# In the first batch the GpSimd queue loads the values ahead of the weights

## The chip, the cores and the metric

One core of one Trainium2 chip. The metric is the device time of one execution, in microseconds (us); lower is better. The traced execution of the kernel before took 487.22 us (span on the core 485.4). Times inside a trace count from the start of its span. The granted clock is the share of its full clock that TensorE was given.

## The reference

Cosine attention (8 batches, 12 heads, 448 positions, head size 64), then a feed-forward block with exact GELU on the 3584 x 768 result:

```python
q_n = q / (norm(q) + 1e-6);  k_n = k / (norm(k) + 1e-6)
attn = softmax(q_n @ k_n.T / tau)
x = (attn @ v)                        # to [3584, 768]
h = x @ w_in                          # 768 x 2048
out = (0.5 * h * (1 + erf(h / sqrt(2)))) @ w_out    # 2048 x 768
```

Inputs and output are float32. The kernel multiplies in bf16.

## The kernel before

The kernel handles two heads at a time (a "group"; six per batch, 48 in all). While TensorE works on attention of batch b, it fills its gaps with the second product of batch b - 1. In batch 0 there is no such work, so it runs dummy matmuls ("spin") to keep its clock up. Tile names in the profile: qk (q and k), sq (squares), rn (reciprocal norms), qkb (scaled q and k in bf16), tp and qkT (transposed), st (scores), pt (their exponentials), sm (sums), o (attention times v), hp (first product), op (second product), wi and wo (the two weights).

v, wi and wo are cast from float32 to bf16 as they are loaded; all of these loads go out on the GpSimd queue. q and k go out on the SyncE queue (one on ScalarE's).

```python
def load_v(g):                      # 112 KB
    nc.gpsimd.dma_start(out=t, in_=v[b, 2*p:2*p+2].rearrange(...))

def load_wi(i):                     # 768 KB each, four of them
    nc.gpsimd.dma_start(out=wi[:, r:r+n, c], in_=moe_w_in[...].rearrange(...))

def scale(g):                       # q half and k half
    for i, eng in enumerate((nc.vector if g == 0 else nc.gpsimd, nc.gpsimd)):
        eng.tensor_tensor(qkb[:, i]..., t[:, i], rn[:, i]..., ALU.mult)

def attention(b, fill):
    for i in range(HP):             # HP = 6 groups of this batch
        g = b * HP + i
        scores(g, 0)                # (if i == 0 and b > 0: done earlier)
        if b == 0:
            upto(scale, min(i + 2, HP)); roots(min(i + 3, HP + 1))
            upto(square, min(i + 4, HP + 1))
            spin(7 if i == 0 else 3)
        if i > 0:
            sums_one(g - 1)         # batch 0
            values(g - 1, ...)      # o: needs v of group g - 1
        scores(g, 2)
        if b == 0: spin(5 if i == 0 else 2)
        if i < HP - 1: transposes(g + 1)
        if b == 0:
            upto(reduce, min(i + 4, HP + 1))
            upto(load_wi, min(i + 2, 4))
        upto(load_v, g + (3 if b == 0 else 4))
        ...                         # cut

# start of the kernel (cut)
spin(24)
upto(square, 1); upto(reduce, 1); roots(1); upto(square, 2)
upto(scale, 1)
upto(load_v, 1)
upto(load_wi, 1)
upto(reduce, 2); roots(2); transposes(0); spin(5)
...
```

`upto(f, n)` calls f for every index below n that is not yet done.

## Time and profile before

| | before |
|---|---|
| device time, median of 3 runs | 486.55 us (486.14 to 487.27) |
| TensorE busy | 464.7 of 485.4 us (96%) |
| GpSimd busy | 256.7 us (53%) |
| ScalarE busy | 299.1 us (62%) |
| mean granted TensorE clock | 0.989 |

The averages hide where time can be won; the prediction below reads that from the waits and the timelines. In a line of waits stand the total us, how often, and the longest. A line of a timeline gives the start and the length in us, the engine (PE is TensorE, POOL GpSimd, ACT ScalarE, DVE VectorE), the line of the kernel, the operation, what it writes and reads, and how many; a bracket at its end gives the engine's idle time just before it and what ended that. One view is added here, the table of windows of 5 us of the kernel before. Its columns are the window, its length, busy us (and instructions) of PE, PEld, DVE, ACT and POOL, then the granted clock, the DMA share (the time that packets took, as a share of 16 engines' span; it can read above 1) and GB/s.

```profile
20.00:25.00 5.00, 2.73 (x23) 1.26 (x23) 2.63 (x4) 4.03 (x8) 4.83 (x6) 1.00 1.11 235
25.00:30.00 5.00, 0.57 (x4) 0.36 (x6) 0.25 (x1) 0.17 (x1) 4.82 (x6) 0.77 1.19 242
30.00:35.00 5.00, 4.28 (x26) 1.82 (x20) 1.24 (x3) 1.72 (x2) 1.64 (x2) 0.50 1.16 238
35.00:40.00 5.00, 5.00 (x32) 2.12 (x29) 1.30 (x2) 3.83 (x7) 2.50 (x3) 0.70 1.12 235
```

See three things. TensorE is all but idle from 25 to 30 us. The clock is low not in the idle window alone but for the two after it. And GpSimd (the last busy column) is full up to 30 us and has time afterwards.

### The profile page before, as it was taken

What the parts mean: (1) busy time and instruction counts of PE and PEld (TensorE: products, weight loads), DVE (VectorE), ACT (ScalarE), POOL (GpSimd) and SP (SyncE); (2) the same over time, 40 slices, a digit from 0 to 9 for tenths busy, and PEclk for the clock granted to TensorE, in tenths of its full rate; (3) what the DMA queues carried; (4) which work ended last, traced back from release to release, by engine and by line L of the source; (5) the groups of instructions that cost most, each with busy time, mean ns of one, the idle gap of its engine ahead of it and who ended that gap; (6) DMA issues with size and microseconds to landing.
All of it is one profiled execution on the core that took longest, in us unless ns stands there. A gap on an engine that the chain in (4) does not pass through costs nothing.

```text
span 485.4 us, 8032 instructions
## 1 busy us (share of the span) xinstructions
PE 464.7 (96%) x3266; PEld 236.3 (49%) x3266; DVE 156.2 (32%) x228; ACT 299.1 (62%) x447; POOL 256.7 (53%) x248
## 2 busy tenths in 40 slices
PE   8758999999999999999999999999999999999995
PEld 5324454445544555445544555444544555445563
DVE  5323513623153232523145231532144231331021
ACT  4838657774766557775676557875566656885400
POOL 4957908947382835668192744849094472411000
PEclk9969999999999999999999999999999999999999
DMA  9998964672056612664056520575046400331022
GB/s 207 237 238 148 204 94 95 138 187 90 7 110 170 172 37 44 137 144 138 0 101 167 142 85 11 122 183 147 0 90 170 101 20 2 65 106 34 1 65 65
DMA packets 48982, 51.87 MB, mean 107 GB/s; under 512 B 3833, under 2 KB 43825, under 8 KB 48945
## 3 DMA queue, kind: packets, MB, share of 16 engines
q1 hardware_dynamic: 31424, 39.34, 29.4%
q0 software_dynamic: 17280, 11.80, 17.2%
q8 instruction: 25, 0.41, 0.3%
q10 hardware_dynamic: 240, 0.23, 0.1%
q14 instruction: 13, 0.10, 0.1%
HBM read 52.04 MB, written 11.11 MB: 130 GB/s over the span
## 4 chain that ended last, share of the span: by engine, by line
PE 87%; ACT 4%; DMA 3%; POOL 2%; issue 2%; DVE 0%; POOLq 0%; ACTq 0%
PE op L244 30%; PE hp L365 29%; PE st L173 8%; PE o L183 8%; PE tp L162 5%; PE sm L204 3%; DMA v<-in_v_dram 3%; PE sm L216 3%; ACT ln L194 2%; POOL qkb L150 1%; ACT g L389 1%; PE spin L291 1%; DMA qk<-in_k_dram 1%; ACT pt L176 1%; POOL wi L266 0%
## 5 line engine op out<-in xcount | busy, mean ns | idle before, releaser
L176 ACT ACTIVATE pt<-st 112x896 bf16<-112x896 f32 x192 | 164.9, 911 | 42.2 <-PE st L173 41.8
L244 PE MATMUL op<-wo,g 128*128 128x384 bf16 x896 | 160.1, 326 | 0.0
L365 PE MATMUL hp<-x,wi 128*128 128x448 bf16 x768 | 149.1, 352 | 0.5
L389 ACT ACTIVATE g<-hp 128x448 bf16<-128x448 f32 x128 | 66.9, 545 | 74.5 <-PE hp L365 73.9
L244 PEld LDWEIGHTS <-g 128*128 128x128 bf16 x896 | 81.8, 98 | 62.0 <-issue 14.6
L365 PEld LDWEIGHTS <-wi 128*128 128x128 bf16 x768 | 74.1, 98 | 72.1 <-issue 5.4
L150 POOL TENSOR_TENSOR qkb<-qk,rn 112x512 bf16<-112x512 f32 x95 | 97.2, 1049 | 11.1 <-DVE rn L141 10.8
L117 POOL TENSOR_TENSOR sq<-qk 112x1024 f32<-112x1024 f32 x45 | 84.5, 1892 | 0.4
L129 DVE TENSOR_REDUCE nq<-sq 112x16 f32<-112x1024 f32 x47 | 57.1, 1216 | 45.9 <-POOL sq L117 45.7
L139 POOL TENSOR_SCALAR se<-sr 112x48 f32<-112x48 f32 (+2 forms) x18 | 5.5, 308 | 117.8 <-ACT sr L137 117.6
L173 PE MATMUL st<-qkT 64*112 64x448 bf16 x384 | 59.1, 377 | 4.2 <-DVE qkT L163 3.1
L230 POOL TENSOR_TENSOR x<-os,rb 128x448 bf16<-128x448 f32 x28 | 31.2, 1133 | 50.7 <-DMA rb<-rows 41.8
L248 DVE COPY ot<-op 128x384 f32<-128x384 f32 x56 | 30.8, 550 | 77.5 <-PE op L244 75.5
L183 PE MATMUL o<-pt,v 112*64 112x448 bf16 x384 | 45.8, 361 | 5.9 <-DMA v<-in_v_dram 5.9
L163 DVE COPY qkT<-tp 128x896 bf16<-128x896 bf16 x48 | 29.9, 623 | 65.3 <-PE tp L162 65.2
L194 ACT ACTIVATE ln<-sm 128x448 f32<-128x448 f32 x34 | 18.3, 538 | 35.3 <-PE sm L204 21.9
L173 PEld LDWEIGHTS <-qkT 64*112 64x112 bf16 x384 | 19.6, 126 | 39.0 <-issue 30.0
L141 DVE RECIPROCAL rn<-se 112x48 f32<-112x48 f32 (+2 forms) x20 | 7.9, 393 | 86.9 <-POOL se L139 86.8
L104 POOL DMA_DIRECT2D v<-in_v_dram x48 | 34.0, 708 | 2.4 <-DMA rb<-rows 1.3
L183 PEld LDWEIGHTS <-v 112*64 112x64 bf16 x384 | 19.6, 111 | 25.7 <-issue 9.5
L162 PE MATMUL tp<-ident,qkb 112*128 112x112 bf16 x384 | 27.4, 215 | 3.3 <-POOL qkb L150 1.3
L162 PEld LDWEIGHTS <-qkb 112*128 112x128 bf16 x384 | 22.0, 99 | 17.2 <-issue 10.6
(31 smaller groups left out, 168.7 us busy)
## 6 DMA issues: line engine op xcount, KB each, us to landing
qk<-in_q_dram SPq DMA_DIRECT2D x48, 224.0 KB
qk<-in_k_dram SPq DMA_DIRECT2D x47, 224.0 KB
rb<-rows SPq DMA_DIRECT2D x28, 224.0 KB
v<-in_v_dram POOLq DMA_DIRECT2D x48, 112.0 KB, 3.1
wi<-in_moe_w_in_dram POOLq DMA_DIRECT2D x4, 768.0 KB, 13.5
wo<-in_moe_w_out_dram POOLq DMA_DIRECT2D x4, 768.0 KB, 15.1
out_dram<-ot SPq DMA_DIRECT2D x8, 336.0 KB
out_dram<-ot SPq DMA_DIRECT2D x8, 288.0 KB
```

The source lines that it names most:

```text
L104: nc.gpsimd.dma_start(out=t, in_=v[b, 2 * p:2 * p + 2].rearrange("h (p c) d -> p h (c d)", c=NC))
L117: nc.gpsimd.tensor_tensor(sq, t, t, ALU.mult)
L129: nc.vector.tensor_reduce(nq, sq, mybir.AxisListType.X, ALU.add)
L150: eng.tensor_tensor(qkb[:, i].rearrange("p c h d -> p h c d"), t[:, i], rn[:, i].to_broadcast([CS, 2, NC, D]), ALU.mult)
L162: nc.tensor.transpose(tp[:, i, c, :], qkb[:, i, c].rearrange("p h d -> p (h d)"), ident)
L173: nc.tensor.matmul(st[:CS, h, :S], lhsT=qkT[rows, 1, c, :], rhs=qkT[rows, 0, :, :], start=True, stop=True)
L176: nc.scalar.activation(pt, st[:CS, :, :S], AF.Exp, scale=inv_tau)
L183: nc.tensor.matmul(o[h * D:(h + 1) * D, :S], lhsT=v_t[g][:, h, c, :], rhs=pt_t[g, c][:, h, :], start=(c == 0), stop=(c == NC - 1))
L230: eng.tensor_tensor(x_t[b][:, p, :], os_t.pop(g), rb_t.pop(g), ALU.mult)
L244: nc.tensor.matmul(ps[:, :NH], lhsT=g_t[sb][:, kf, t * 128:(t + 1) * 128], rhs=wo[:, kf, ni * NH:(ni + 1) * NH], start=(kf == 0), stop=(kf ...
L365: nc.tensor.matmul(hps[m], lhsT=wi[:, kd, m * 128:(m + 1) * 128], rhs=x_t[b][:, kd, :], start=(kd == 0), stop=(kd == KD - 1))
L389: nc.scalar.activation(g_t[sb][:, m, hf * S:(hf + 1) * S], hps.pop(m), AF.Gelu)
```

## The change

The intent: values are small and needed soon, weights are large and needed after 50 us, and both are on one queue. So v0, v1 and v2 go out first. A tiny copy that reads q of group 0 holds v0 and v1 back until that load is in. In the loop v is asked for one group earlier and stands ahead of wi, and wi starts one iteration later.

```diff
             if b == 0:
                 upto(reduce, min(i + 4, HP + 1))
-                upto(load_wi, min(i + 2, 4))
-            upto(load_v, g + (3 if b == 0 else 4))
+            upto(load_v, g + 4)
+            if b == 0:
+                upto(load_wi, min(i + 1, 4))
@@ start of the kernel
     spin(24)
+    late = nrm.tile([CS, 1], F32, tag="late", name="late", bufs=1)
+    nc.gpsimd.tensor_copy(late, qk_t[0][:, 0, 1, NC - 1, D - 1:D])
+    upto(load_v, 2)
     upto(square, 1)
     ...
     upto(scale, 1)
-    upto(load_v, 1)
-    upto(load_wi, 1)
+    upto(load_v, 3)
```

## The prediction

> **What bounds the kernel now.** I read the page first. TensorE (PE) is busy for 96% of the span, so time can only be won where PE stands idle or runs slowly. The slices show where that is: of 40 slices of 12.1 us, only the first four are below 9 tenths, and the third (24 to 36 us) has a granted clock of 6 tenths.
>
> ```profile
> PE   8758999999999999999999999999999999999995
> PEclk9969999999999999999999999999999999999999
> DMA  9998964672056612664056520575046400331022
> ```
>
> Next the waits of PE over the whole span. One stands out, and it occurs once:
>
> ```profile
> PE o L183 <- DMA v<-in_v_dram: 5.9, 1, 5.9
> PE st L173 <- DVE qkT L163: 3.1, 5, 0.7
> PE spin L291 <- POOL ident masks.py:199: 1.3, 1, 1.3
> PE tp L162 <- POOL qkb L150: 1.3, 2, 0.9
> ```
>
> The timeline of PE places it. The product of group 1 with its values (o) starts 5.93 us late, at 29.43, and that group of eight then takes 1.70 us where the same eight take 0.92 us for the next head pair:
>
> ```profile
> 22.55 0.95 PE L204 MATMUL sm<-pt,ones 112*64 112x448 bf16 x8
> 29.43 1.70 PE L183 MATMUL o<-pt,v 112*64 112x448 bf16 x8 [5.93 <-DMA v<-in_v_dram]
> ...
> 38.07 0.92 PE L183 MATMUL o<-pt,v 112*64 112x448 bf16 x8
> ```
>
> The timeline of GpSimd (POOL) says why the values are late. POOL issues both the weights wi and the values v. The values of groups 1 and 2 are issued at 16.58, behind two 768 KB pieces of wi (issued at 9.85 and 15.75), and the tile view of v gives 12.8 and 13.5 us from their issue to landing; where nothing lies ahead of them (issue at 39.59) it gives 3.2 us.
>
> ```profile
> 9.85 0.80 POOL L266 DMA_DIRECT2D wi<-in_moe_w_in_dram  x1
> 10.65 2.07 POOL L150 TENSOR_TENSOR qkb<-qk,rn 112x512 bf16<-112x512 f32 x2
> ...
> 15.75 0.83 POOL L266 DMA_DIRECT2D wi<-in_moe_w_in_dram  x1
> 16.58 1.33 POOL L104 DMA_DIRECT2D v<-in_v_dram  x2
> 17.93 2.05 POOL L150 TENSOR_TENSOR qkb<-qk,rn 112x512 bf16<-112x512 f32 x2
> 20.07 0.25 POOL L139 TENSOR_SCALAR se<-sr 112x16 f32<-112x16 f32 x1
> 20.40 1.89 POOL L117 TENSOR_TENSOR sq<-qk 112x1024 f32<-112x1024 f32 x1
> ```
>
> The chain that ended last agrees: it runs over a piece of 12.80 us "DMA v" from 16.58 to 29.39.
>
> **What the Trainium skill says.** "DMA: Bandwidth & Descriptors", section "Queues, rings and completion order": on each DMA engine a queue's descriptors are consumed in ring order, and the engine goes round between queues that have work. The trace agrees: v behind two wi pieces takes 12.8 us, v alone 3.2 us. So order of issue on the POOL queue is the lever. The same page, "SWDGE vs HWDGE vs iDMA": a transfer that changes its type can only be issued from GpSimd; v and wi both go from float32 to bf16, so they share that queue and can only be reordered. "TensorE: Matmul & The Clock Gate", section "What's actually happening": after an idle window of about 3.4 us the matmul clock drops to half and it needs sustained work to come back. The trace agrees: the windows of 5 us have a granted clock of 0.77, 0.50 and 0.70 at 25 to 30, 30 to 35 and 35 to 40 us, and 1.00 on both sides.
>
> **The change part by part.**
>
> Added: one tiny copy on POOL that reads the last element of q of group 0, so it waits until that load is in (VectorE starts on it at 4.33). Then v0 and v1 are issued, 0.7 to 0.9 us each: POOL has done that by about 6.5, and its first real work (qkb of group 0) starts at 7.51. This lies in idle time and costs nothing. Their landing is needed at 17.70 (o of group 0) and 23.5 (o of group 1). The first loads compete with the q and k loads, but even the 8.4 us that v0 took in this crowd before puts them at about 13 and 15. In time.
>
> Moved: v2 follows scale of group 0 and the first wi is no longer there (9.05 to 10.65 now holds v0 and wi0). It moves into the loop, one wi in each of iterations 0 to 3. So iteration 3 now carries a wi issue (0.83 us) which it did not before.
>
> Removed: the wait of 5.93 us. With it goes the slow clock. Between 29.43 and 37.5 the groups ran at 1.70 (o), 0.99 (st), 0.99 (spin), 0.95 (tp), 0.99 (st), 1.37 (spin), 1.57 (sm); at full clock the timeline gives 0.92, 0.59, 0.59, 0.57, 0.59, 0.78, 0.95. The difference is 0.78 + 0.40 + 0.40 + 0.38 + 0.40 + 0.59 + 0.62 = 3.6 us. So 9.5 us are on the path, plus up to 0.6 from POOL waits.
>
> **But it is not all given back, because POOL becomes the pace of the first batch.** An iteration (score to score of the next group) takes PE and ScalarE 5.07 us when nothing disturbs it (41.13 to 46.20). POOL takes, from qkb to qkb, 23.76 - 17.93 = 29.59 - 23.76 = 5.83 us: two qkb 2.05, se 0.25, sq 1.89, wi 0.83, v 0.68, gaps 0.13. Until now the wait for v hid that. After the change POOL does the same work in iterations 1 to 3. Let me lay it out. se of group 2 stays at 13.59 (it waits for ScalarE). sq to 15.75, v3 and wi0 (0.70 + 0.83) to 17.3, qkb of group 2 to 19.4. Then 5.83 each: qkb of group 3 to 25.2, of 4 to 31.0, of 5 to 36.9. PE transposes each as it comes (tp of group 2 came right behind qkb at 20.04 before). PE's own pace from 19.6 would have been 24.7, 29.8, 34.9, so POOL is what ends last, by 0.5, 1.2 and 2.0 us. The transposes of group 5 start at 44.93 before and at 36.9 after: 8.0 us earlier. After that nothing in batch 0 needs POOL for PE, and the 7.5 us from there to the first hp matmul (52.45) stay: hp starts at 44.4.
>
> **Are the weights still there in time?** Behind one another a wi piece moves at the 0.16 MB/us that the software queue got between 17 and 25 us beside the q and k loads, so 0.786 MB in 4.9 us, less than the 5.83 us between issues. wi0 to wi3 are issued at about 16.5, 22, 28 and 34 and land by about 23, 29, 35 and 42. The first half of the columns (wi0, wi1) is needed at 44.4, the second half 48 matmuls of 0.19 us later, 53.5. The wo pieces, issued from 45.74 before, go out from about 39 and need 4 times 4.9 us: to about 62. The first half is needed at 71.85 - 8 = 64. So it holds. The rest of the kernel is PE at full clock with waits under 1 us, and it moves as one piece.
>
> The sum: 486.55 - 8.0 = 478.5 us, 1.6% less.
>
> **The rivals.**
>
> First: POOL does not bind, and the whole 9.5 us (or 10.1 with the waits for qkb) come back: 476.5 to 477. For it: the iterations from 41 us on run at 5.07 without a wait for POOL. Against it: POOL has no idle time from 13.6 to 31.6 in the timeline, apart from gaps under 0.1 us; in that stretch it is at its own pace.
>
> Second: a new DMA wait. The trace shows that under load the software queue moved nothing until about 14.9 us, though v0 was issued at 9.0, while q and k had all of the 235 GB/s. If v0 and v1 are held back in the same way, they land at about 17 to 18 and o of group 0 waits up to 1 us; or if they do share early, 2 times 112 KB (0.9 us each) push q and k of groups 2 and 3 back from 8.6 and 10.5 to some 10.4 and 13.2, right at their squares (9.77 and 13.92). Either would cost 0.3 to 1.5 us: 479 to 480.
>
> Third: wi, now 6 us later, is late for hp, or wo for the second product. By the count above there are 10 and 2 us of slack; if the DMA engines were slower than I think, PE would wait a few us and the clock might fall again: 482 to 485. DMA is not saturated from 40 to 50 us before (132 and 100 GB/s), which speaks against it.
>
> Fourth: the first batch's idle gaps, now 1.5 of 5.83 us, let the clock fall. PE had gaps of 0.39 + 0.72 us per iteration at 20 us and stayed at 1.00; I give it little.
>
> **Range and chances.** 478.5 is the POOL-paced case (some seven in ten). The free case is 2 us below, the small DMA costs 0.5 to 1.5 us above, the noise of a run about 0.5 us. Range 476.9 to 480.6. Faster by over 2% means below 476.8, which is about all that the wait, the clock and the POOL waits hold together: 0.06. Slower needs the weights to be late by far more than the slack: 0.01.
>
> **What would show each step.** Right: no wait of o for v; clock 9 in every slice from the second on; POOL without idle time from 13.6 to about 37 and PE waiting for qkb some 0.5 to 0.8 us before each tp of groups 3, 4 and 5; tp of group 5 near 36.9, hp near 44.4, and after that the same timeline shifted by 8. Wrong: a wait of hp for wi or of op for wo; a wait of sq for q or k, or of o for v, early on; iterations of 5.1 us with idle POOL, which is the free case.

## The result and the profile after

| | before | after |
|---|---|---|
| device time, median | 486.91 us (486.14 to 487.48, 4 runs) | 479.28 us (478.96 to 479.29, 4 runs) |
| ratio | | 0.9843 (95%: 0.9826 to 0.9860) |
| mean granted clock, traced run | 0.989 | 0.999 |
| first hp matmul | 52.45 us | 44.13 us |
| TensorE wait of o for v | 5.93 us | none |
| TensorE wait of tp for qkb | 1.3 us, 2 times | 3.6 us, 5 times |

1.6% faster. Of the 8.2 us between the two spans, 8.3 had been gained by the first hp matmul; the rest of the kernel is the same work.

The waits of TensorE over the whole span of the changed kernel (total, times, longest):

```profile
PE st L173 <- DVE qkT L163: 3.9, 6, 0.7
PE tp L162 <- POOL qkb L150: 3.6, 5, 1.1
PE spin L291 <- POOL ident masks.py:199: 1.3, 1, 1.3
PE sm L204 <- ACT pt L176: 0.4, 1, 0.4
```

The wait for v is gone from the list, and the wait of the transposes for GpSimd's scaling has grown by 2.3 us. Three waits in the timeline of TensorE of the changed kernel are 1.6 us of that; another of 1.08 us, before the transposes of group 0, cost nothing (they began at 8.97 us, at 9.10 before).

```profile
22.68 0.92 PE L183 MATMUL o<-pt,v 112*64 112x448 bf16 x8
...
25.07 0.57 PE L162 MATMUL tp<-ident,qkb 112*128 112x112 bf16 x8 [0.43 <-POOL qkb L150]
...
30.88 0.57 PE L162 MATMUL tp<-ident,qkb 112*128 112x112 bf16 x8 [0.57 <-POOL qkb L150]
...
36.71 0.57 PE L162 MATMUL tp<-ident,qkb 112*128 112x112 bf16 x8 [0.58 <-POOL qkb L150]
```

o of group 1 takes 0.92 us at full clock, right behind its sums. The transposes of groups 3, 4 and 5 stand 5.81 and 5.83 us apart. The timeline of GpSimd of the changed kernel has the same spacing and no gap for anything but its own work:

```profile
16.34 0.78 POOL L266 DMA_DIRECT2D wi<-in_moe_w_in_dram  x1
17.12 2.07 POOL L150 TENSOR_TENSOR qkb<-qk,rn 112x512 bf16<-112x512 f32 x2
19.27 0.25 POOL L139 TENSOR_SCALAR se<-sr 112x16 f32<-112x16 f32 x1
19.60 1.89 POOL L117 TENSOR_TENSOR sq<-qk 112x1024 f32<-112x1024 f32 x1
21.44 0.73 POOL L104 DMA_DIRECT2D v<-in_v_dram  x1
22.16 0.78 POOL L266 DMA_DIRECT2D wi<-in_moe_w_in_dram  x1
22.93 2.08 POOL L150 TENSOR_TENSOR qkb<-qk,rn 112x512 bf16<-112x512 f32 x2
```

Note how small the waits are beside what they stand for: 0.4 to 0.6 us each in the list, while the iteration is 0.76 us longer than the 5.07 us it takes undisturbed. A wait is counted only from the end that is modelled for the matmul before; the spacing of one operation from iteration to iteration is the safer reading.

And the windows of 5 us of the changed kernel, to set against those of before: no low clock, and GpSimd full throughout.

```profile
25.00:30.00 5.00, 4.22 (x37) 2.07 (x37) 2.63 (x4) 3.98 (x8) 4.83 (x7) 1.00 1.12 241
30.00:35.00 5.00, 3.71 (x33) 1.72 (x31) 2.63 (x4) 4.08 (x8) 4.83 (x6) 1.00 1.12 220
```

### The profile page after: what moved, and what is told of

It is laid out like the page before. It is cut to its first block, busy times and chain, and to the rows that moved or that the text cites. A ratio compares the mean times of both kernels' runs of the same rounds, so it can differ in the third digit from the quotient of the medians. Undisturbed runs are those within 1.5% of the kernel's fastest.

```text
span 477.2 us, 8032 instructions
## 1 busy us (share of the span) xinstructions
PE 460.2 (96%) x3266; PEld 234.6 (49%) x3266; DVE 156.6 (33%) x228; ACT 299.1 (63%) x447; POOL 257.6 (54%) x249
## 4 chain that ended last, share of the span: by engine, by line
PE 87%; ACT 5%; POOL 3%; DMA 2%; DVE 1%; issue 1%; POOLq 0%; ACTq 0%
PE op L244 31%; PE hp L366 30%; PE st L173 8%; PE o L183 8%; PE tp L162 5%; PE sm L204 3%; PE sm L216 3%; ACT ln L194 2%; DMA qk<-in_q_dram 2%; POOL qkb L150 1%; ACT g L390 1%; POOL sq L117 1%; ACT pt L176 1%; PE spin L291 1%; DVE qkT L163 0%
## 5 line engine op out<-in xcount | busy, mean ns | idle before, releaser
L163 DVE COPY qkT<-tp 128x896 bf16<-128x896 bf16 x48 | 29.9, 623 | 54.7 <-PE tp L162 54.4
```

## The experiments

The theory: order in the GpSimd queue made v1 late (5.93 us), the idle time then cost a slow clock (3.6 us), and GpSimd's own pace takes part of that back. The rivals: v was late because the DMA engines were full; the clock costs nothing of its own; GpSimd's waits only stand in for others. Eleven runs, five rounds each. e1 to e4 ran on one chip beside 11 runs of the kernel before (487.06 us median, 483.95 to 489.23), e5 to e8 on another (487.97, 484.74 to 489.25), the last three again on the first chip, later (486.87, 483.25 to 487.71, 5 runs).

### e1: the wait kept, the clock kept up

The kernel before, with

```diff
+                if g == 2:
+                    spin(28)
                 values(g - 1, not one)
```

> The kernel before, with 28 extra spin matmuls ahead of the product of group 1 with its values (28 times 0.195 = 5.5 us of work in the wait). The wait for v stays, only the clock is kept up. Theory (the loss was a wait of 5.93 us plus 3.6 us of half clock after it): the slow groups between 29.4 and 37.5 us go back to full clock, 3.6 us gained, 483.2 us; granted clock 0.99 or more. Rival (the clock costs nothing of its own, as GpSimd would set the pace in that stretch anyway): less than 1 us gained, 486 us.

Measured: 483.26 us median (483.15 to 483.65), ratio 0.9927 (0.9897 to 0.9958), granted clock 1.000. From the timeline of TensorE of e1:

```profile
23.19 5.50 PE L291 MATMUL spin<-blank,ident 112*112 112x448 bf16 x28
28.62 0.95 PE L183 MATMUL o<-pt,v 112*64 112x448 bf16 x8
...
48.10 12.88 PE L367 MATMUL hp<-x,wi 128*128 128x448 bf16 x66
```

5.5 us of useless matmuls make the kernel 3.8 us faster than the kernel before beside it (medians). o still starts 5.4 us after the end of its sums (22.31 + 0.95), but takes 0.95 us instead of 1.70. Not all of the 3.8 us need be the clock: in this execution v of group 1 had landed at 27.6 us (29.4 in the trace of the kernel before), so o waited for the spins, not for v, and started 0.8 us earlier. From o of group 1 to the first hp matmul the kernel before takes 23.02 us (29.43 to 52.45) and e1 19.48 us. So the slow clock is a cost of its own: 3.5 us by this stretch, 3.6 us by the sum of the stretched groups.

The second thing to see is the spread: 0.5 us for e1, 5.3 us for the kernel before in the same rounds. Over all 27 runs of the kernel before beside the experiments, the time rises as the mean granted clock falls: four runs at 0.993 or 0.996 average 484.6 us, six at 0.983 or 0.984 average 488.4. But fourteen runs at 0.989 lie anywhere from 484.69 to 488.45, so the clock is not all of it. The landing of v varies too, and the spins of e1 hide that. How much each contributes is not shown; these runs were not traced.

### e2: half of the scaling moved off GpSimd

The changed kernel, with

```diff
-        for i, eng in enumerate((nc.vector if g == 0 else nc.gpsimd, nc.gpsimd)):
+        for i, eng in enumerate((nc.vector if g < HP else nc.gpsimd, nc.gpsimd)):
```

> The changed kernel, with the q half of the scaling of groups 1 to 5 on VectorE instead of GpSimd. Theory (GpSimd paces the first batch at 5.83 us an iteration, which takes back some 2 us of the gain): GpSimd is lighter by 0.5 to 1.05 us an iteration, the waits of tp for qkb of groups 3, 4 and 5 go, iterations become 5.1 us, 1.5 to 2.2 us gained on the changed kernel, 477.1 to 477.8 us. Rival (the 0.4 to 0.6 us waits for qkb only replace waits for ScalarE that come right after): no gain, 479 us.

Measured: 477.16 us median (477.07 to 477.44), ratio 0.9801 (0.9771 to 0.9831). From the timeline of TensorE of e2:

```profile
24.63 0.56 PE L162 MATMUL tp<-ident,qkb 112*128 112x112 bf16 x8
...
29.70 0.56 PE L162 MATMUL tp<-ident,qkb 112*128 112x112 bf16 x8
...
34.88 0.56 PE L162 MATMUL tp<-ident,qkb 112*128 112x112 bf16 x8
```

No bracket, so no wait, and 5.07 and 5.18 us between them; hp starts at 42.29 against 44.13. GpSimd's pace was worth 2.1 us: the changed kernel gave 479.25 on the same chip later (the control below). One thing cost part of what was moved: with VectorE on the q half at the same time, GpSimd's k half takes 1.31 to 1.54 us where it took 1.04. The Trainium skill, "SBUF — State Buffer", section "🔬 SBUF: two separate sides", says that VectorE with two SBUF inputs and GpSimd share a port pair that one of them locks for a whole instruction. The longer times agree with that: VectorE's half (0.68 us) started first each time, and overlaps of 0.40, 0.64, 0.47 and 0.41 us went with 0.27, 0.50, 0.33 and 0.27 us more for GpSimd. That is an agreement, not a test of the cause.

### e3: two wi issues moved into GpSimd's idle time

The changed kernel, with wi0 issued after v2 and wi1 after the scaling of group 1:

```diff
+                if i == 0:
+                    upto(load_wi, 2)         # right after scale of group 1
...
-                upto(load_wi, min(i + 1, 4))
+                upto(load_wi, min(i + 2, 4) if i else 2)
...
     upto(load_v, 3)
+    upto(load_wi, 1)
```

> The changed kernel, with the first two pieces of wi issued in GpSimd's idle time before and after the scaling of group 1 (9.6 and 12.4 us), so that the loop holds two issues of wi and not four, still behind v0 to v2. Theory (GpSimd time paces iterations 1 to 3): 2 times 0.78 us less up to the scaling of group 5, transposes of group 5 at 35.2 instead of 36.7, 1.5 us gained on the changed kernel, 477.8 us. Rival (the pieces of wi, 6 us earlier, take DMA time from q and k of groups 3 and 4, or from v3): a wait of sq for q or k, or of o for v, and no gain or a loss, 479 us or more.

Measured: 477.99 us median (477.80 to 478.30), ratio 0.9818 (0.9788 to 0.9848). From the timeline of TensorE of e3:

```profile
30.33 0.57 PE L162 MATMUL tp<-ident,qkb 112*128 112x112 bf16 x8 [0.41 <-POOL qkb L150]
...
35.40 0.56 PE L162 MATMUL tp<-ident,qkb 112*128 112x112 bf16 x8
```

The transposes of group 5 come at 35.40, where 35.2 was expected (36.71 in the changed kernel). Issuing a transfer is work for GpSimd: two issues of 0.78 us out of the loop are 1.3 us off the kernel (medians, control below). wi0 and wi1 going out 6.6 and 9.6 us earlier hurt nothing: v0 to v2 were ahead of them, and no wait for v, q or k came in the loop.

### e4: only v0, v1 and v2 ahead of the first wi

The kernel before, with `upto(load_v, 1)` at the start turned into `upto(load_v, 3)` and nothing else.

> The kernel before with one part of the change alone: v0, v1 and v2 are issued ahead of the first piece of wi; the loop (a piece of wi, then v of three groups ahead) and the start are as before. Same bytes, about the same times, other order. Theory (order in the GpSimd queue made v1 late): o of group 1 does not wait; v3 and v4 are now behind pieces of wi, land at about 35 and 41, against a need at 34 and 40, so waits of 0 to 3 us in all, 479.5 to 483 us. Rival (the DMA engines were full, so v is late in any order): o of group 1 still waits 3 us or more, 484 us or more.

Measured: 480.87 us median (480.15 to 481.87), ratio 0.9881 (0.9847 to 0.9916). From the timeline of TensorE of e4:

```profile
22.95 0.92 PE L183 MATMUL o<-pt,v 112*64 112x448 bf16 x8
...
34.85 0.95 PE L183 MATMUL o<-pt,v 112*64 112x448 bf16 x8 [0.36 <-DMA v<-in_v_dram]
...
41.18 0.95 PE L183 MATMUL o<-pt,v 112*64 112x448 bf16 x8 [1.07 <-DMA v<-in_v_dram]
```

The same bytes, with the DMA engines as full, and o of group 1 does not wait: it was the order, not the load. (v1 and v2 are also issued some 7 us earlier here, which e4 alone does not separate from the order; e8 does.) v3 and v4, still behind pieces of wi, took 12.4 and 12.9 us to land; they were in at 34.8 and 41.1, as expected, and cost 0.4 and 1.1 us. This one line brings most of the gain; the rest of the change brings 1.6 us more (480.87 against 479.25, the control).

### e5: without the copy that holds v0 and v1 back

The changed kernel without the two `late` lines, so that v0 and v1 go out at 1.5 us.

> The changed kernel without the small copy that holds v0 and v1 back until q of group 0 is in: they are issued at about 1.4 us. Theory A (the copy is needed: v competes with q and k of groups 0 and 1, 2 times 112 KB): VectorE's first square (4.2 us) or ScalarE's square of group 1 (6.7 us) starts 0.5 to 1 us later, and all of the rest with it: 479.8 to 480.3 us. Theory B (under load the GpSimd queue first moves data about 5 us after the issue, as in both kernels, so v comes after group 0 anyway): start unchanged, 479.2 to 479.4 us.

Measured: 479.52 us median (479.29 to 480.61). In its trace VectorE's first square began at 4.66 us, against 4.20 in the changed kernel, which looked like theory A. So it was run again beside the control.

### e6: e2 and e3 together

> The changed kernel with both earlier experiments at once: the q half of the scaling on VectorE, and two wi issues in GpSimd's idle time. Theory (with the first of these GpSimd is no longer the bound, TensorE and ScalarE are, at 5.07 to 5.17 us an iteration): the two gains of 1.8 and 1.0 us do not add; 0.0 to 0.3 us better than the first alone, 476.9 to 477.2 us. Rival (GpSimd is still the bound): the second gain adds, 476.1 us or less.

Measured: 477.24 us median (477.16 to 477.54), against 477.16 for e2 on the other chip. The gains of 2.1 and 1.3 us do not add: both relax the same bound, and once it no longer binds the second is worth nothing. GpSimd now waits for ScalarE in every iteration (0.33 to 1.04 us). GpSimd's busy time from 15.7 to 36 us fell from 19.64 us in e2 to 17.18 us in e6, and hp started at 42.27 against 42.29.

### e7: e6 with fewer spins

```diff
-                spin(7 if i == 0 else 3)
+                spin(4 if i == 0 else 1)
...
-                spin(5 if i == 0 else 2)
+                spin(1)
```

> The same with both, and most of the idle spin matmuls of the first batch taken out (7, 5, 3 and 2 become 4, 1, 1 and 1). Theory (what paces the first batch now is ScalarE, busy 4.8 us of 5.07, with TensorE's spins filling its waits[...]): 0.7 to 1.7 us gained on the kernel with both, 475.4 to 476.4 us, clock 0.99 or more. Rival (the spins keep the clock up): the granted clock falls in the first batch and the time rises to 478 us or more.

Measured: 475.39 us median (475.21 to 475.61, 5 runs), ratio 0.9748 (0.9722 to 0.9775), granted clock 1.000: 1.85 us better than e6, a little more than the range expected. This is the fastest version, and the only one clearly more than 2% faster than the kernel before. From the table of windows of e7, its four iterations from the scores of group 1 to those of group 5 (columns as above):

```profile
14.96:34.38 19.42, 15.79 (x138) 7.90 (x138) 13.34 (x20) 18.67 (x33) 18.43 (x21) 1.00 1.15 241
```

4.86 us an iteration, with ScalarE busy for 18.67 of 19.42 us (96%). GpSimd is nearly as busy (18.43 us), but no transpose waits for it in this stretch, while score matmuls wait for ScalarE's exponentials; two of three such waits in the timeline of TensorE of e7:

```profile
19.58 0.40 PE L173 MATMUL st<-qkT 64*112 64x448 bf16 x2 [0.81 <-ACT pt L176]
20.38 0.40 PE L173 MATMUL st<-qkT 64*112 64x448 bf16 x2 [0.41 <-ACT pt L176]
```

The pace has gone from GpSimd to TensorE's own spins and from there to ScalarE. With the stall gone the kernel had more spins than it needed. Whether the kernel before could have done with fewer was not tested.

### e8: wi ahead of v inside the loop again

```diff
-            upto(load_v, g + 4)
             if b == 0:
                 upto(load_wi, min(i + 1, 4))
+            upto(load_v, g + 4)
```

> The changed kernel with the order inside the loop turned back: in each of iterations 0 to 3 the piece of wi is issued ahead of v (v is still asked for four groups ahead, and v0 to v2 still come first). Theory (what matters is how many pieces of wi are queued ahead of v compared with when it is needed): v3 is now behind wi0, v4 behind wi0 and wi1, landing at about 26 and 32 against a need at 34 and 40: no wait for v, 479.3 us as the changed kernel. Rival (the order within the iteration is what saves it): waits for v3 or v4 of over 1 us, 480.5 us or more.

Measured: 480.07 us median (479.13 to 480.62). No wait of o for v in the trace, though v3 to v5, each with a piece of wi just ahead of it, took 9.0 to 9.1 us to land against 4.4 to 4.6 in the control: order in the queue costs v about 4.5 us at the same lead, and asking for it four groups ahead covers that. But 0.8 us over the changed kernel, between the two theories. The trace shows the loss before 12 us, where the programs are the same: ScalarE's square of group 1 waited 1.06 us for k. So it was run again beside a control.

### The control, e8 and e5 again

> The changed kernel unchanged, as a control on one chip with the two that follow. Expected: 479.3 us, 478.9 to 480.4.

> The kernel of e8_swap again, whose profiled run lost 1.1 us before 12 us, where its program is still the same as the changed kernel's. Theory (that is a run's own variation in when k of group 1 lands): within 0.4 us of the control, and from the transposes of group 1 to the first hp matmul 29.8 to 29.9 us as in the changed kernel. Rival (the order in the loop costs 0.6 us or more): 0.6 us or more over the control, and that stretch is longer.

> The kernel of e5_no_late again, beside the control. If the copy that holds v0 and v1 back is worth what the first profile showed (first square 0.4 us later): 0.3 to 0.5 us over the control. If it is worth nothing: within 0.2 us of it.

Measured on one chip: the changed kernel 479.25 us (478.96 to 480.05), e8 again 479.22 (479.06 to 479.40), e5 again 479.14 (479.02 to 479.70). All three are the same. The stretch from the transposes of group 1 to the first hp matmul is 29.9 us in all of them (14.94 to 44.81, 14.47 to 44.37, 14.38 to 44.26). So neither the order inside the loop nor the `late` copy is worth anything that these runs can see. What remains is a variation of about 1 us from run to run in when the first q and k land; the control's own trace has it too (square of group 1 at 7.48 us, against 6.70 in the first trace of the changed kernel and 7.92 in that of e8). The first results of e5 and e8 fit that variation. They ran on the other chip, where the changed kernel itself was not run, so a difference between the chips is not excluded. The lesson is to run a control before a difference of half a microsecond is explained.

## Why the prediction was right

The time was 479.28 us, 0.8 above the 478.5 predicted and inside the range.

- **The bound, and what is removed.** Right. The wait for v went, and with it the low clock. e4 shows that it was the order; e1 shows that the clock was a cost of its own, 3.5 us from o of group 1 to hp (3.8 us between the medians) where 3.6 was predicted.
- **What is added is free.** Right: v0 and v1 were issued from 4.88 us, before the first scaling at 7.37, and landed after 7.8 to 8.4 us, so by about 14 us, in time for 17.57. The copy that holds them back turned out not to be needed (e5 again, 479.14 us).
- **GpSimd becomes the pace.** Right, and the heart of it. Transposes of groups 3, 4 and 5 were predicted at 25.2, 31.0 and 36.9 and came at 25.07, 30.88 and 36.71; hp was predicted at 44.4 and came at 44.13. The waits for qkb were 0.43 to 0.58 us, a little under the 0.5 to 0.8 forecast. That this pace took part of the gain back is shown by e2: with it gone, 2.1 us more, which brings the ratio to 0.9801, at the 2% line and not clearly past it.
- **The weights are in time.** Right: the four pieces of wi landed at 24.2, 29.9, 36.0 and 42.8 (predicted 23, 29, 35 and 42), the four of wo by 62.2 (predicted 62), and no wait for wi or wo appears.
- **The rivals.** The free case did not come; e2 is what it would look like (477.16). Late v or late q and k: no wait of o for v came. Of q and k, waits of up to 1 us occurred in some runs, but before any of v had moved (e8 and the control: first packets of v after 9 us), so they don't speak for the rival. A clock that falls in the gaps: no, 1.00 in every window of the first batch, and in e7 too.
- **Slips that changed nothing.** Not only the first four slices of TensorE are below 9 tenths; the last, the kernel's end, is too (5 before and after). And in the second rival 10.5 us pushed back by two v of 0.9 us is 12.3, not 13.2; the squares of groups 2 and 3 began at 9.64 and 13.79 us, no later than before (9.77 and 13.92).
- **Where the 0.8 us are.** Not in a step of the mechanism, as far as the traces show, but in the sum's starting point. The saving of 8.0 us was read from a trace of an execution that took 487.22 us, and subtracted from the median of other executions, 486.55. Taken from its own execution it gives 479.2. The kernel before varies from 483.25 to 489.25 us from run to run and the changed kernel by about 1 us, so the saving varies too. That the one traced execution lay near the median was luck, and the number came out this close in part because of it.

## What to carry to other kernels

GpSimd's queue served its transfers in order (v took 12.8 us behind two pieces of wi, 3.2 us with nothing ahead): put the small transfer that is needed soon ahead of the large one that is needed late, on whichever queue has to carry both, and count what lies ahead of it in time, not in number. Before you add up what a removed wait gives back, lay out the next engine's own pace for that stretch: a loaded engine that was hidden by the stall (here GpSimd, 5.83 us an iteration against 5.07) takes its share, and its small listed waits understate it. And a stall of TensorE can cost a slow clock after it as well (here 5.9 us of stall, then 3.5 us); once such a stall is gone, the number of filler matmuls is worth trying again.

## What the Trainium skill lacked or had wrong

- "DMA: Bandwidth & Descriptors" gives about 1 us to the first byte on the GpSimd path and packet-wise turns between queues. Beside the q and k loads of the start, the GpSimd queue moved nothing for about 3 to 6 us: v0 issued at 8.99 us, first packets between 14 and 15 us (before); issued at 4.88, first packets between 9 and 10 (after); issued at 1.51, two packets between 4 and 5 and the bulk after 5 (e5). Once both moved, they did take turns, as the page says: 76 packets each between 18 and 19 us in the kernel before. Where the first microseconds go is not settled here. The same page calls the generation of descriptors small; here each issue of v or wi took 0.66 to 0.87 us of GpSimd, one of each is a quarter of its iteration of 5.83 us, and moving two of them was worth 1.3 us.
- "TensorE: Matmul & The Clock Gate" has the clock come back after about 3.4 us of sustained work. After the idle 5.93 us the granted clock of the kernel before was at half from about 27.8 to 37.9 us (windows of 0.2 us), so for 8.4 us after work began again at 29.43, with TensorE busy but for one gap of 0.72 us. The page also puts the cost of warming up below 1% of a kernel. That held: 3.5 us, 0.7% of 487. Gaps of 0.6 to 0.7 us, with TensorE busy for 3.7 of 5 us (74%), kept the clock at 1.00 (changed kernel, 30 to 35 us).
